# Clustered attention before two MLPs, one core: operands of the scores laid out as [hi; lo] and [hi; one-hot; maxima], and the first heads reordered

## Chip, core, metric

The kernel runs on one core of one Trainium2 chip. The metric is the device time of one execution in microseconds (us); lower is better.

## What is computed

Attention over 2 batches of 8 heads, 768 tokens, head size 64, where a query sees only keys of its own cluster, then two MLPs over the 1536 rows of 512 that the heads make together:

```python
q_assign = argmax(einsum('bhsd,hcd->bhsc', q_n, c_n), -1)   # nearest of 16 centroids of the head
k_assign = argmax(einsum('bhsd,hcd->bhsc', k_n, c_n), -1)
mask = q_assign[..., :, None] == k_assign[..., None, :]
scores = where(mask, scale * q @ k.T, -1e9)
attn = exp(scores - max(scores)); attn = attn / (sum(attn) + 1e-9)
x = (attn @ v) as rows of 512
h = x @ w_in;  x = (h * sigmoid(1.702 * h)) @ w_out                        # 2048 wide
out = (silu(x @ w_gate) * (x @ w_val)) @ w_out2                            # 1536 wide
```

All data are float32 in the reference; the kernel's inputs are laid out by the host without arithmetic.

## The kernel before

Every product on PE (TensorE) that must be accurate takes its operands as hi + lo, where hi carries the bits that one pass of the array keeps. Attention goes head by head, 16 heads; the two MLPs follow. Five pairs of operand tiles `q2`, `k2` go round among the heads, and a written-out order sets what each engine does (the scheduler keeps the program's order on all five engines).

What one head h needs, in the names used below:

- **Load and convert.** `load_qk` (L302) brings q and k, transposed, into a staging tile, twice over (one copy for the hi rows, one for the lo rows): 768 KB and 384 KB on the SP queue, two staging tiles. `hi_q`, `hi_k` (L319, L322) round them on ACT (ScalarE); `lo_q`, `lo_k` (L325, L329) take the difference, on DVE (VectorE) or, for the first heads, on POOL (GpSimd). This is done four heads ahead.
- **Clusters.** `similar` (L415): eight products per head of queries and keys with the centroids (`sims`). `largest` and `assign` (L440, L455): a chain of some nine operations on DVE that turns the similarities into one-hot rows, which are copied under the operands. From the fifth head on two heads go through it together.
- **Maxima.** `smax` (L490): 12 products and 12 reductions on DVE (`nm`), the largest score of each query; `mneg` (L508) and `mrow` (L525) or, for the first two heads, `mrow_at_once` (L512) put minus the maxima as a row under the queries, by a small transfer or by 6 tiny products and two copies on ACT.
- **Scores.** `scores` (L537): 12 pairs of products (`st`), each followed by Exp on ACT into `p`. Maxima of head h + 1 are mixed among them.
- **Values.** `pv` (L554): 36 products of `p` with the values (72 instructions), six at a time.

A score's first product takes 112 rows (hi and lo of half the sizes, one-hot rows at 96), its second 97 (the row of maxima at 96). `keep_warm` (L340, L344) issues products that nothing uses; they fill PE while it waits. The order of the first heads is in L606 to L634 and in the branches `if h == 0`, `if h == 1` of the loop over heads (L637 on): the one-hot chains of heads 0, 1, 2 and 3 go one head at a time.

Of the kernel before, what the change touches and what calls it, by code (L numbers as in the profile page):

```python
# [25 lines left out]
def tile_cluster_attention_two_mlps(ctx: ExitStack, tc: tile.TileContext, qk, v, cen, w1, w2, wg, wv, w3, out):  # L26
# [62 lines left out]
    # weights in the order of their first use  # L89
# [28 lines left out]
    def take_in():  # L118
        """Takes the weights in, one after the other, in steps of one operation of VectorE."""
# [18 lines left out]
    # the two MLPs, by parts of a batch's tokens  # L138
# [4 lines left out]
    def split_w(it):  # L143
        """A weight's split, as two thunks."""
# [26 lines left out]
    def first_products(b, f, p, names, tanh_scale):  # L171
        """Thunks: the first products of a part, through the activation."""
# [79 lines left out]
    def run(s1_thunks, splits, steps):  # L252
        """One part's or unit's thunks, the splits of later weights and `steps` of taking weights in, mixed."""
# [18 lines left out]
    with ExitStack() as att:  # attention  # L272
# [29 lines left out]
        def load_qk(h):  # L302
            b, hh = divmod(h, H)
            src = qk[b, hh].rearrange("d t s -> d (t s)")
            to = stage[h % 2].rearrange("p a t s -> p a (t s)")
            nc.sync.dma_start(out=to[0:64], in_=src.unsqueeze(1).to_broadcast([D, 2, 2 * S]))
            nc.sync.dma_start(out=to[64:96], in_=src.rearrange("(a p) s -> p a s", a=2))

        def load_first():
            src = qk[0, 0].rearrange("d t s -> d (t s)")  # L310
            to = stage[0].rearrange("p a t s -> p a (t s)")
            nc.sync.dma_start(out=to[0:64, 0], in_=src)
            nc.sync.dma_start(out=to[64:96], in_=src.rearrange("(a p) s -> p a s", a=2))
# [471 lines left out]
```

## Time and profile before

| what | value |
|---|---|
| timed runs | 870.86, 872.61, 872.85 us; median 872.61 us |
| profiled execution | span 869.7 us from its first to its last instruction; its time with what lies around the span is not listed apart |
| PE | busy 853.4 us (98%) |
| DVE, ACT, POOL | busy 605.8 us (70%), 431.9 us (50%), 30.9 us (4%) |
| granted clock of PE, mean | 0.991 |
| chain that ended last | PE 94%, DVE 4%, DMA 1% |
| loads of q and k | 15 issues of 768 KB and 17 of 384 KB; all traffic 61.92 MB |

The span runs from the first to the last instruction of the core. Attention takes about the first 300 us of it, the MLPs the rest. Busy time counts an engine's own instructions; PE's matmuls overlap, so that the start of one matmul after another tells its pace, not its duration. The granted clock of 1.00 is PE's upper level (2.4 GHz), 0.5 its lower (1.2 GHz); a stretch between them had some of both. Idle time of an engine is told with what ended it.

### The profile page before, as it was taken

The page shows a single profiled execution, that of the slowest core. Times are in us where ns is not written, and L with a number is a line of the kernel's source. Part 1 is how long each engine was busy: PE and PEld are TensorE (multiplying, and loading weights), DVE is VectorE, ACT ScalarE, POOL GpSimd, SP SyncE. Part 2 cuts the span into 40 slices and gives each one's busy share as a digit, 9 for nine tenths or more (in the row PEclk, how much of TensorE's full clock was granted, in tenths as well). Part 3 has the DMA queues.
Part 4 walks back from the last instruction along what each step waited for, and adds up shares of the span by engine and source line. Part 5 has one row for each costly group of instructions (what it writes and reads, how often), then busy time and mean ns, then how long its engine had stood idle before and what let it go on. Part 6 is the DMA issues. An engine that isn't in the chain of part 4 may idle for free.

```text
span 869.7 us, 12993 instructions
## 1 busy us (share of the span) xinstructions
PE 853.4 (98%) x5108; PEld 766.9 (88%) x5108; DVE 605.8 (70%) x1116; ACT 431.9 (50%) x809; POOL 30.9 (4%) x46
## 2 busy tenths in 40 slices
PE   6989999999999999999999999999999999999998
PEld 5789999999999888888888888888888888888886
DVE  7978889889897468888887677687773344334433
ACT  5645675575574555665665546454442233222322
POOL 5530000000000000000000000000000000000000
PEclk8989999999999999999999999999999999999999
DMA  7454633633122023323222222222200010000001
GB/s 160 105 119 114 150 99 91 154 70 91 46 63 88 5 73 109 110 100 120 98 98 73 74 83 73 87 74 72 97 1 1 1 49 25 1 1 1 0 1 73
DMA packets 28340, 61.92 MB, mean 71 GB/s; under 512 B 14756, under 2 KB 14840, under 8 KB 28280
## 3 DMA queue, kind: packets, MB, share of 16 engines
q1 hardware_dynamic: 27416, 59.53, 23.8%
q10 hardware_dynamic: 864, 1.57, 0.5%
q8 instruction: 40, 0.66, 0.3%
q14 instruction: 20, 0.16, 0.1%
HBM read 57.31 MB, written 3.15 MB: 70 GB/s over the span
## 4 chain that ended last, share of the span: by engine, by line
PE 94%; DVE 4%; DMA 1%; issue 0%; ACT 0%; SPq 0%; DVEq 0%
PE h L156 39%; PE a L156 27%; PE pv L559 14%; PE st L543 8%; PE smax L495 4%; PE sims L423 3%; PE xt L588 1%; DVE T L450 1%; DVE nm L500 1%; DMA st<-in_qk 1%; DVE T L452 0%; DVE q L389 0%; DVE oT L469 0%; DVE T L443 0%; DVE T L465 0%
## 5 line engine op out<-in xcount | busy, mean ns | idle before, releaser
L156 PE MATMUL h<-xh,sp 128*128 128x512 f32 (+1 forms) x1280 | 327.1, 337 | 0.1
L156 PEld LDWEIGHTS h<-xh,sp 128*128 128x128 f32 x1280 | 223.2, 189 | 28.5 <-issue 0.3
L156 PE MATMUL h<-xl,sp 128*128 128x256 f32 (+1 forms) x640 | 215.9, 337 | 0.0
L188 DVE SCALAR_TENSOR_TENSOR t<-t,h 128x512 f32<-128x512 f32 x112 | 61.8, 552 | 161.0 <-ACT t L185 161.0
L185 ACT ACTIVATE t<-h 128x512 f32<-128x512 f32 x112 | 54.7, 488 | 204.4 <-PE h L156 204.4
L156 PE MATMUL a<-g,sp 128*128 128x512 f32 (+1 forms) x768 | 139.4, 337 | 0.0
L156 PEld LDWEIGHTS a<-g,sp 128*128 128x128 f32 x768 | 119.9, 189 | 16.7
L559 PEld LDWEIGHTS pv<-v,p 128*128 128x128 f32 x1152 | 134.2, 192 | 0.2 <-issue 0.2
L559 PE MATMUL pv<-v,p 128*128 128x65 f32 x1152 | 133.9, 273 | 0.0
L156 PEld LDWEIGHTS h<-xl,sp 128*128 128x128 f32 x640 | 120.9, 189 | 14.3
L550 ACT ACTIVATE p<-st 128x384 f32<-128x384 f32 x192 | 90.8, 491 | 33.3 <-PE st L543 26.1
L156 PE MATMUL a<-sp,g 128*128 128x512 f32 x432 | 106.1, 390 | 0.0
L500 DVE TENSOR_REDUCE nm<-smax 128x1 f32<-128x384 f32 x192 | 100.1, 555 | 7.5 <-PE smax L495 7.4
L543 PE MATMUL st<-q,k 112*128 112x384 f32 (+1 forms) x384 | 100.3, 350 | 0.0
L150 DVE TENSOR_TENSOR sp<-w,sp 128x512 fp32r<-128x512 f32 x136 | 92.8, 684 | 5.2 <-ACT sp L149 5.1
L156 PEld LDWEIGHTS a<-sp,g 128*128 128x128 f32 x432 | 79.6, 188 | 15.6
L149 ACT CAST sp<-w 128x512 fp32r<-128x512 f32 x136 | 83.1, 614 | 0.0
L197 DVE TENSOR_TENSOR g<-t,g 128x512 fp32r<-128x512 f32 x112 | 62.0, 553 | 16.1 <-ACT g L194 11.5
L543 PEld LDWEIGHTS st<-q,k 112*128 112x128 f32 (+1 forms) x384 | 69.8, 193 | 1.9 <-ACT p L550 0.4
L495 PE MATMUL smax<-k,q 112*128 112x384 f32 x192 | 65.5, 351 | 5.3 <-ACT q L472 4.2
L194 ACT CAST g<-t 128x512 fp32r<-128x512 f32 (+1 forms) x48 | 24.7, 514 | 81.2 <-DVE t L193 81.2
L190 ACT CAST g<-t 128x512 fp32r<-128x512 f32 x64 | 32.9, 514 | 31.3 <-DVE t L188 31.3
(94 smaller groups left out, 687.4 us busy)
## 6 DMA issues: line engine op xcount, KB each, us to landing
raw<-in_w SPq DMA_DIRECT2D x44, 512.0 KB, 3.4
st<-in_qk SPq DMA_DIRECT2D x15, 768.0 KB, 6.1
st<-in_qk SPq DMA_DIRECT2D x17, 384.0 KB, 6.2
raw<-in_wg SPq DMA_DIRECT2D x12, 512.0 KB, 3.4
raw<-in_wv SPq DMA_DIRECT2D x12, 512.0 KB, 3.5
v<-in_v SPq DMA_DIRECT2D x16, 192.0 KB, 3.0
out<-osb ACTq DMA_DIRECT2D x6, 256.0 KB
out<-osb SPq DMA_DIRECT2D x6, 256.0 KB, 2.1
```

What stands on the lines that cost most here:

```text
L149: lambda: nc.scalar.copy(t[:, 0, :], w),
L150: lambda: nc.vector.tensor_tensor(out=t[:, 1, :], in0=w, in1=t[:, 0, :].bitcast(F32), op=ALU.subtract),
L156: nc.tensor.matmul(out=out_ps, lhsT=lhs[a], rhs=rhs[b], start=(start and j == 0), stop=(stop and j == 2), **kw)
L185: nc.scalar.activation(t, hs[0], ACTF.Tanh, scale=tanh_scale)
L188: nc.vector.scalar_tensor_tensor(out=t, in0=t, scalar=1.0, in1=hs[0], op0=ALU.add, op1=ALU.mult)
L190: nc.scalar.copy(g[:, 0, at], t)
L197: nc.vector.tensor_tensor(out=g[:, 1, at], in0=t, in1=g[:, 0, at].bitcast(F32), op=ALU.subtract)
L495: nc.tensor.matmul(out=ps, lhsT=q2(h)[:, 1, c * 128:(c + 1) * 128], rhs=k2(h)[:, 1, n * HALF:(n + 1) * HALF],)
L500: nc.vector.tensor_reduce(out=nm_t[h][:, c, n:n + 1], in_=ps, axis=AX.X, op=ALU.max)
L543: nc.tensor.matmul(out=ps, lhsT=k2(h)[0:rows, a, c * 128:(c + 1) * 128], rhs=q2(h)[0:rows, a, at], start=(a == 1), stop=(a == 0),)
L550: nc.scalar.activation(p_t[h, c][:, at], ps, ACTF.Exp, scale=scale)
L559: nc.tensor.matmul(out=pv_t[h][:, i, :], lhsT=p[:, i * 128:(i + 1) * 128], rhs=v_t[h % 3][:, c, :], start=(c == 0 and i == 0), stop=(c == ...
```

## The change

The operands are held in tiles of 128 rows. Slot 0 is [q_hi; q_lo] against [k_lo; k_hi], 64 rows each; slot 1 is [q_hi; one-hot at 64; zeros; row of maxima at 96] against [k_hi; one-hot; zeros; ones]. So a score is one product on 128 rows and one on 97; `smax` takes 80 rows of slot 1, and `sims` 128 rows in place of 96; the number of products is the same. Each head is loaded once (384 KB, one issue) into one of four staging tiles; head 0's q comes on the ACT queue. `hi_k` becomes two casts on ACT; `lo_q` is 64x768 where it was 32x1536. POOL clears rows 64 to 96 of slot 1 in all ten operand tiles (`extra_rows`). DVE sets `wd`, which POOL did.

The order of the first heads is written anew: head 0's maxima are taken in two halves, each followed at once by its row (`mrow_at_once(0, n)`) and half of head 0's scores; head 1's clusters come between the two halves; heads 2 and 3 go through the one-hot chain together, during head 0's products with the values; head 1's maxima row goes by the transfer. Two stretches of products that nothing uses are shorter or gone (20 to 16, 10 to none). `lo_q(4)` and `lo_k(4)` go to DVE, from POOL.

```diff
-        q2_t = [(qk1_p if i == FIRST else qk_p).tile([112, 2, S], F32R, name=f"q2_{i}") for i in range(NQK)]
-        stage = [st_p.tile([96, 2, 2, S], F32, name=f"st{i}") for i in range(2)]
+        q2_t = [(qk1_p if i == FIRST else qk_p).tile([128, 2, S], F32R, name=f"q2_{i}") for i in range(NQK)]
+        NST = 4
+        stage = [st_p.tile([D, 2, S], F32, name=f"st{i}") for i in range(NST)]
+        ONE, MROW = D, 96
...
         def load_qk(h):
-            nc.sync.dma_start(out=to[0:64], in_=src.unsqueeze(1).to_broadcast([D, 2, 2 * S]))
-            nc.sync.dma_start(out=to[64:96], in_=src.rearrange("(a p) s -> p a s", a=2))
+            nc.sync.dma_start(out=stage[h % NST], in_=qk[b, hh])
...
         def load_first():
+            for i, eng in ((1, nc.sync), (0, nc.scalar)):
+                eng.dma_start(out=stage[0][:, i, :], in_=qk[0, 0, :, i, :])
...
         def hi_q(h):
-            nc.scalar.copy(q2(h)[0:96], stage[h % 2][:, :, 0, :])
+            nc.scalar.copy(q2(h)[0:D], src.to_broadcast([D, 2, S]))
         def hi_k(h):
-            nc.scalar.copy(k2(h)[0:96], stage[h % 2][:, :, 1, :])
+            nc.scalar.copy(k2(h)[0:D, 1, :], src)
+            nc.scalar.copy(k2(h)[D:2 * D, 0, :], src)
...
+        def extra_rows(i):
+            for t in (q2_t[i], k2_t[i]):
+                nc.gpsimd.memset(t[D:MROW, 1, :].bitcast(F32), 0.0)
+            nc.gpsimd.memset(k2_t[i][MROW:MROW + 1, 1, :].bitcast(F32), 1.0)
...
         def scores(h, c, n):
-            for a, rows in ((1, 112), (0, 97)):
+            for a, rows in ((0, 2 * D), (1, MROW + 1)):
...
         sims = similar([0])
-        keep_warm(20)
+        keep_warm(16)
-        hi_q(1)
         hi_k(1)
-        lo_q(1, nc.gpsimd)
-        lo_k(1, nc.gpsimd)
-        load_qk(3)
+        hi_q(1)
         dummy = sm_p.tile([128, 1], F32, tag="dummy", name="dummy")
         nc.scalar.activation(dummy, y0, ACTF.Exp)
         do(largest([0], sims))
-        do(assign([0], (nc.scalar.copy, nc.vector.tensor_copy)))
-        hi_q(2)
+        do(assign([0], (nc.scalar.copy, nc.gpsimd.tensor_copy)))
+        lo_k(1, nc.gpsimd)
+        lo_q(1, nc.gpsimd)
         hi_k(2)
-        lo_q(2, nc.gpsimd)
+        extra_rows(2)
         lo_k(2, nc.gpsimd)
         load_qk(4)
         for i, (c, n) in enumerate((c, n) for m in range(2) for n in range(2) for c in range(3 * m, 3 * m + 3)):
             smax(0, c, n, *((ps_m, "m"), (ps_m, "m"), (ps_s, "s"), (ps_s, "s"), (ps_s, "s"))[i % 5])
-            if i == 4:
-                sims = similar([1])
-        mneg(0)
-        keep_warm(10)
-        mrow_at_once(0)
+            if i == 5:
+                mneg(0, slice(0, SC // 2))
+        mrow_at_once(0, 0, ps_o, "o")
+        mneg(0, slice(SC // 2, SC))
+        for c in range(SC):
+            scores(0, c, 0)
+        sims = similar([1])
+        mrow_at_once(0, 1, ps_o, "o")
         do(largest([1], sims))
-        do(assign([1], (nc.vector.tensor_copy, nc.vector.tensor_copy)))
+        do(assign([1], (nc.vector.tensor_copy, nc.gpsimd.tensor_copy)))
+        hi_q(2)
+        for c in range(SC):
+            scores(0, c, 1)
+        lo_q(2, nc.gpsimd)
+        hi_k(3)
+        lo_k(3, nc.gpsimd)
+        hi_q(3)
+        lo_q(3, nc.gpsimd)
+        for t in v_t[1:]:
+            nc.gpsimd.memset(t[:, :, D:D + 1], 1.0)
+        for i in range(3, NQK):
+            extra_rows(i)
         for h in range(NH):
...
-                        eng = nc.vector if h else nc.gpsimd
-                        lo_q(h + 4, eng)
-                        lo_k(h + 4, eng)
+                        lo_q(h + 4)
+                        lo_k(h + 4)
...
-                    if c == 2:
+                    if c == 3:
                         mneg(1)
-                        sims = similar([2])
-                        mrow_at_once(1)
-                        do(largest([2], sims))
-                        do(assign([2], (nc.scalar.copy, nc.vector.tensor_copy)))
-                if h == 1 and c == 1:
-                    do(largest([3], similar([3])))
-                    do(assign([3]))
+                        sims = similar([2, 3])
+                        mrow(1, ps_o, "o")
+                        do(largest([2, 3], sims))
+                        do(assign([2, 3]))
```

The order that comes of it, at three places. In the rows q_0 to q_4 and k_0 to k_4 are the operand tiles of heads 0 to 4 (and then of 5 to 9 again), st_120 to st_123 the staging tiles, and a row's x counts equal instructions that follow each other.

PE, from head 0's maxima to its products with the values, before:

```order
L495 MATMUL smax<-k_0_112,q_0_107 128x384 x7
L344 MATMUL warm<-xh_70 128x512 x10
L519 MATMUL mrow_348<-ident,nr 1x128 x3
L519 MATMUL mrow_353<-ident,nr 1x128 x3
L543 MATMUL st<-q_0_107,k_0_112 128x384 x14
L495 MATMUL smax<-k_1_113,q_1_108 128x384
```

and in the change:

```order
L353 MATMUL warm<-xh_70 128x512 x16
L502 MATMUL smax<-k_0_112,q_0_107 128x384 x12
L525 MATMUL mrow_319<-ident,nr 1x128 x3
L549 MATMUL st<-q_0_107,k_0_112 128x384 x12
L430 MATMUL sims<-k_1_113,cs 128x384 x2
L430 MATMUL sims<-q_1_108,cs 128x384 x2
```

Head 0's first scores stand right behind half of the row of maxima, and head 1's similarities, which stood between the maxima, behind those scores.

ACT, around head 0's Exps (L550, L556), before:

```order
L523 CAST q_0_107<-mrow_353 1x384
L550 ACTIVATE p<-st 128x384 x12
L320 CAST q_3_110<-st_121 96x1536
L323 CAST k_3_115<-st_121 96x1536
L320 CAST q_4_111<-st_120 96x1536
L323 CAST k_4_116<-st_120 96x1536
```

and in the change:

```order
L529 CAST q_0_107<-mrow_364 1x384
L321 CAST q_2_109<-st_122 64x1536
L556 ACTIVATE p<-st 128x384 x6
L325 CAST k_3_115<-st_123 64x768
L326 CAST k_3_115<-st_123 64x768
L321 CAST q_3_110<-st_123 64x1536
L321 CAST q_4_111<-st_120 64x1536
L325 CAST k_4_116<-st_120 64x768
L326 CAST k_4_116<-st_120 64x768
```

Head 2's `hi_q` now stands ahead of the second six Exps; the casts of heads 3 and 4 still follow the last Exp.

DVE, from head 1's one-hot rows to its maxima, before:

```order
L469 STREAM_TRANSPOSE oT<-T 64x384
L472 CAST q_1_108<-oT 16x384
L472 CAST k_1_113<-oT 16x384
L500 TENSOR_REDUCE nm<-smax 128x1 x12
L510 TENSOR_REDUCE nr<-nm 128x6
```

and in the change:

```order
L476 STREAM_TRANSPOSE oT<-T 64x384
L479 CAST q_1_108<-oT 16x384
L330 TENSOR_TENSOR q_4_111<-st_120,q_4_111 64x768
L336 TENSOR_TENSOR k_4_116<-st_120,k_4_116 64x768
L507 TENSOR_REDUCE nm<-smax 128x1 x12
L518 TENSOR_REDUCE nr<-nm 128x6
```

Head 4's `lo_q` and `lo_k` (L330, L336), which stood on POOL, now stand on DVE ahead of the 12 reductions of head 1's maxima.

## Rows read from the trace of the kernel before

**Rows 1.** Windows of the whole core: stretch, busy us (x instructions) by engine, clock, DMA share, GB/s.

```profile
50.00:55.00 5.00, 2.31 (x10) 1.97 (x10) 4.53 (x9) 1.62 (x4) 0.82 (x1) 0.77 1.11 215
55.00:60.00 5.00, 5.00 (x19) 5.00 (x18) 2.99 (x6) 2.59 (x6) 0.00 (x0) 0.55 0.69 143
...
100.00:150.00 50.00, 49.99 (x369) 49.55 (x367) 43.92 (x83) 30.97 (x55) 0.00 (x0) 1.00 0.47 117
...
200.00:250.00 50.00, 49.98 (x376) 49.64 (x374) 43.95 (x84) 31.02 (x55) 0.00 (x0) 1.00 0.22 56
```

**Rows 2.** Timeline of PE to 60 us: start, duration, line, work, idle before.

```profile
1.46 3.90 PE L344 MATMUL warm<-xh 128*128 128x512 f32 x9 [1.46 <-DVE y L348]
...
13.10 0.84 PE L423 MATMUL sims<-k,cs 96*128 96x384 f32 x2
13.74 0.84 PE L423 MATMUL sims<-q,cs 96*128 96x384 f32 x2
...
22.58 1.46 PE L495 MATMUL smax<-k,q 112*128 112x384 f32 x5 [1.52 <-ACT q L472]
...
29.46 1.47 PE L519 MATMUL mrow<-ident,nr 128*1 128x128 f32 x12
30.86 3.05 PE L543 MATMUL st<-q,k 112*128 112x384 f32 x14
...
38.12 1.45 PE L559 MATMUL pv<-v,p 128*128 128x65 f32 x12
...
53.43 0.69 PE L495 MATMUL smax<-k,q 112*128 112x384 f32 x1 [2.69 <-ACT q L472]
```

**Rows 3.** Timeline of PE from 60 us on.

```profile
64.88 0.59 PE L423 MATMUL sims<-k,cs 96*128 96x384 f32 x2
...
66.35 1.45 PE L559 MATMUL pv<-v,p 128*128 128x65 f32 x12
68.39 0.58 PE L423 MATMUL sims<-k,cs 96*128 96x384 f32 x2 [0.59 <-DVE T L443]
...
75.20 0.60 PE L543 MATMUL st<-q,k 112*128 112x384 f32 x2
...
83.01 6.86 PE L559 MATMUL pv<-v,p 128*128 128x65 f32 x60
```

**Rows 4.** Timeline of DVE to 62 us.

```profile
15.62 2.65 DVE L450 TENSOR_TENSOR T<-T,mx 128x192 f32<-128x192 f32 x1
18.38 1.81 DVE L452 TENSOR_TENSOR T<-T,wd 128x192 f32<-128x192 f32 x1
...
22.02 0.35 DVE L472 CAST k<-oT 16x384 fp32r<-16x384 f32 x1
...
23.40 5.66 DVE L500 TENSOR_REDUCE nm<-smax 128x1 f32<-128x384 f32 x12
...
30.79 0.36 DVE L452 TENSOR_TENSOR T<-T,wd 128x192 f32<-128x192 f32 x1
...
31.96 0.92 DVE L465 TENSOR_SCALAR T<-T,s,s 128x192 f32<-128x192 f32 x1
```

**Rows 5.** Timeline of POOL to 62 us.

```profile
14.60 3.46 POOL L327 TENSOR_TENSOR q<-st,q 32x1536 fp32r<-32x1536 f32 x1 [6.00 <-ACT q L320]
...
30.68 2.09 POOL L648 MEMSET k<- 1x768 f32 x3
```

**Rows 6.** Groups by line and shape: engine, work, count, busy us, mean ns, idle before.

```profile
L331 DVE TENSOR_TENSOR k<-st,k 64x768 fp32r<-64x768 f32 x11 | 10.5, 951 | 8.8 <-ACT k L323 8.7
L331 POOL TENSOR_TENSOR k<-st,k 64x768 fp32r<-64x768 f32 x5 | 9.1, 1819 | 0.6 <-ACT k L387 0.3
...
L480 ACT CAST k<-oT 16x768 fp32r<-16x768 f32 x6 | 5.0, 829 | 0.1
...
L450 DVE TENSOR_TENSOR T<-T,mx 128x384 f32<-128x384 f32 x6 | 3.3, 558 | 0.2
...
L387 ACT CAST k<-st 64x1536 fp32r<-64x1536 f32 x1 | 1.5, 1476 | 1.1 <-DMA st<-in_qk 1.1
```

More of the change, by code (lines that the diff above doesn't have):

```diff
@@ L337, in tile_cluster_attention_two_mlps @@
         load_v(0)
+        load_qk(2)
+        load_qk(3)
         zeros = xh[0][:, 0, 0:512]
@@ L379, in tile_cluster_attention_two_mlps @@
         nc.vector.reciprocal(y1, y1)
-        cn = acst.tile([128, 2, 96], F32, name="cn")
-        for a in range(2):
-            nc.vector.tensor_scalar(out=cn[:, a, 0:64], in0=craw, scalar1=y1, scalar2=None, op0=ALU.mult)
-            nc.vector.tensor_scalar(
-                out=cn[:, a, 64:96], in0=craw[:, 32 * a:32 * a + 32], scalar1=y1, scalar2=None, op0=ALU.mult
-            )
-        first = stage[0][0:64, 0:1]
-        nc.scalar.copy(k2(0)[0:64], first[:, :, 1, :].to_broadcast([64, 2, S]))
@@ L388, in tile_cluster_attention_two_mlps @@
-        nc.scalar.copy(q2(0)[0:64], first[:, :, 0, :].to_broadcast([64, 2, S]))
-        nc.vector.tensor_copy(q2(0)[64:96], stage[0][64:96, :, 0, :])
-        lo_k(0, nc.gpsimd)
-        ctp = ps_x.tile([96, 2, 128], F32, tag="x", name="ctp")
-        keep_warm(9)
-        for a in range(2):
-            nc.tensor.transpose(out=ctp[:, a, :], in_=cn[:, a, :], identity=ident)
-        ch = acst.tile([96, 2, 128], F32R, name="ch")
-        cl = acst.tile([96, 2, 128], F32R, name="cl")
+        cn = acst.tile([128, 2, D], F32, name="cn")
@@ new lines, in tile_cluster_attention_two_mlps @@
+        nc.vector.tensor_scalar(
+            out=cn, in0=craw.unsqueeze(1).to_broadcast([128, 2, D]), scalar1=y1, scalar2=None, op0=ALU.mult
+        )
+        ctp = ps_x.tile([128, 128], F32, tag="x", name="ctp")
+        keep_warm(9)
+        nc.tensor.transpose(out=ctp, in_=cn.rearrange("p a d -> p (a d)"), identity=ident)
+        keep_warm(5)
+        ks, qs = stage[0][:, 1, :], stage[0][:, 0, :]
+        nc.vector.tensor_copy(k2(0)[0:D, 1, :], ks)
+        nc.scalar.copy(q2(0)[0:D, 0, :], qs)
@@ L408, in tile_cluster_attention_two_mlps @@
-        for n in range(2):
-            at = slice(n * HALF, (n + 1) * HALF)
-            t = q2(0)[64:96, :, at]
-            nc.vector.tensor_tensor(out=t, in0=stage[0][64:96, :, 0, at], in1=t.bitcast(F32), op=ALU.subtract)
+        for i, src, r in ((0, ch, slice(0, 2 * D)), (1, cl, slice(0, D)), (2, cl, slice(D, 2 * D))):
+            to = cs[r, i, LEAD:].rearrange("p (h x) -> p h x", x=128)[:, :, 0:NC]
+            nc.scalar.copy(to, src[r].rearrange("p (h c) -> p h c", c=NC))
+        lo_k(0)
@@ L412, in tile_cluster_attention_two_mlps @@
+        lo_q(0)
+        nc.scalar.copy(q2(0)[0:D, 1, :], qs)
         ident_r = acst.tile([128, 128], F32R, name="ident_r")
@@ L531, in mrow @@
             nc.sync.dma_start(
-                out=q2(h)[96:97, 0, :].rearrange("p (c s) -> p c s", s=128).bitcast(F32), in_=row.bitcast(F32)
+                out=q2(h)[MROW:MROW + 1, 1, :].rearrange("p (c s) -> p c s", s=128).bitcast(F32), in_=row.bitcast(F32)
             )
@@ L546, in scores @@
                     rhs=q2(h)[0:rows, a, at],
-                    start=(a == 1),
-                    stop=(a == 0),
+                    start=(a == 0),
+                    stop=(a == 1),
                 )
@@ L639, in tile_cluster_attention_two_mlps @@
             maxima = list(steps) if more else []
-            for i, step in enumerate(steps):
+            for step in steps if h else ():
                 scores(h, *step)
-                if maxima and (h > 0 or i >= 6):
+                if maxima:
                     next_smax(h + 1, maxima)
             if h == 0:
-                for t in v_t[1:]:
-                    nc.gpsimd.memset(t[:, :, D:D + 1], 1.0)
-                for t in k2_t[2:]:
-                    nc.gpsimd.memset(t[96:97, 0, :].bitcast(F32), 1.0)
-                hi_q(3)
-                hi_k(3)
-                lo_q(3, nc.gpsimd)
-                lo_k(3, nc.gpsimd)
                 load_qk(5)
```

96 lines of the change are left out of this document (44 added, 52 removed).

## Prediction

> **What bounds the kernel now.** I read the windows of the core first, then PE's timeline, then DVE's and POOL's timelines where PE waits, then the groups for durations. From 100 us on PE is busy 49.99 of 50 us [rows 1]: there it sets the pace and waits for nobody, and the change leaves its number of products alone. So what the change is worth lies before, up to head 2's first score, at 75.20 us [rows 3]; behind it I move the rest of the kernel as one block. Up to there PE's timeline shows what holds it: head 0's maxima start at 22.58, its scores at 30.86, its products with the values at 38.12, head 2's maxima at 53.43 after 2.69 us idle [rows 2]. The profiled span is 869.7 us; that execution's own time isn't listed, and the median of the runs, 872.61, stands 2.9 above the span. I keep that distance and forecast by the shift of the 75.20. A difference of 0.3%, about what can be told from none, is 2.6 us.
>
> **The steady part: nothing.** Per head `hi_k` is two casts of 0.83 us on ACT for one of 1.48, `lo_q` on DVE goes to 0.95 (rows of the same shape as `lo_k` now) [rows 6]: both engines have room beside PE (31 and 44 of 50 us [rows 1]). Where that cover were gone, ACT's 0.2 us a head would be 3 us in all. The loads fall to a third, but PE doesn't wait for them.
>
> **Head 0 to its first score.** PE's nine fillers end at 5.36 [rows 2], a transposition and three short DVE operations follow; I estimate four times 0.35, the cast of [rows 4]: 6.8. Then `lo_k`, `lo_q`, 0.95 each [rows 6]: 8.7. Six of the eight similarities wait for them; at 0.18 each (1.47 for eight, 64.88 to 66.35 [rows 3]) the chain on DVE starts at 10.1. Before, it was 14.6 (13.74 + 0.84 [rows 2]). The chain took 7.4 us to the first cast at 22.02, because two of its operations took 2.65 and 1.81 where such a one takes 0.36 [rows 4]. POOL's subtraction ran from 14.60 to 18.06, and the first of them ended at 18.27 [rows 5, 4]: DVE was held till POOL's instruction was done. The change puts POOL's subtractions behind the chain: 7.4 - 3.7 = 3.7, to 13.8. The first half's cast for k is now POOL's; no row shows one, so between DVE's 0.35 and half of POOL's subtraction of twice the size, 0.91 [rows 4, 6]; I take 0.6 (it reads one operand, not two). The second half is 0.6 later, but the first maxima need the first alone: start at 14.6, 8.0 us early. Reductions go at 0.47 (5.66 for 12 [rows 4]); the first ends near 15.4, and the small reduction after six, the seventh, and the last product that needs its buffer bring 18.8. Half a row of maxima is 0.73 (1.47 for both [rows 2]), its copy on ACT 0.5 by an estimate from 0.83 for twice the columns [rows 6]: **scores from 20.0, where it was 30.86, a lead of 10.9 us.**
>
> **The beginning's new work on POOL.** The memset of rows 64 to 96 is three times 0.70 for each pair of tiles [rows 5], two pairs of them ahead of the chain, beside DVE's first operations. Beside such memsets a DVE operation with two inputs took 0.36, as always, and one with a single input and scalars 0.92, ending 0.1 after the memset [rows 4, 5]. So I charge `lo_k`, `lo_q` nothing and the copy of k0 at most 0.7, which the fillers on PE cover in part. Were all held, 2.1 us would be added to the 14.6. The Trainium skill, SBUF — State Buffer, section "Who interferes with whom", says the same with a reason: a VectorE instruction with two SBUF inputs is kept off by a GpSimd one that reads SBUF, not by one that only writes, and one in a two-port mode by either. By that rule the sum stays as it is without the 2.1, and the rule speaks against the change further on: subtractions of both engines exclude each other.
>
> **Head 0's scores and values.** Six pairs at 0.436 (3.05 for seven [rows 2]): 22.6. Head 1's similarities 1.47: 24.1. The second half of the row, 0.73, and its copy: 25.3. On ACT `hi_q(2)` stands in front of the second Exps, 1.48 [rows 6]: 26.8, and six Exps at the pairs' pace end at 29.4. PE's last pair is out at 28.5; values from 28.5, where it was 38.12: lead 9.6.
>
> **The new wait.** DVE's 12 reductions for head 1 stand behind `lo_q(4)`, `lo_k(4)`, and these behind ACT's casts: after the last Exp k(3), two of 0.83, q(3) and q(4), 1.48 each, to 34.0 [rows 6]. POOL, free at 30.2 after its last cast, does three subtractions of 1.82 [rows 6], to 35.7; its third and DVE's `lo_q(4)` want the same moment, and one waits for the other as in [rows 4, 5]. Either way three operations follow each other from 33.8: 1.82 + 2 x 0.95 = 3.7, **37.5**. Had they not excluded each other, 35.9. PE meanwhile does six products of `pv` with 12 instructions at 0.11 (6.86 for 60 [rows 3]), three maxima, six more, and stops at 31.7 for want of a PSUM buffer till the first reduction ends, 38.0: **6.3 us idle, where before nothing stopped here.**
>
> **Heads 1 to 3.** Reductions to 43.3 or so (12 x 0.47), mneg, 16 similarities 2.9: 46.4. The chain for two heads at once is nine operations at 0.56 [rows 6]: 51.6; two casts of 0.83: head 2's maxima at 53.5. Before: 53.43. **The lead is spent.** PE has two blocks of values, the row and a pair of scores to do after the similarities, some 3.1 us, so it idles 4 us. The SP queue isn't late: head 1's row goes out behind `load_qk(6)`, which waits for POOL's `lo_q(2)` near 32 and is past by 46. From 53.43 to 75.20 before passed 21.8 us, in them head 3's similarities of their own (1.47) and a wait for DVE's buffer, 0.59 [rows 3], which are gone: 19.7.
>
> **The clock.** After the 2.69 us idle at 53.4 the granted clock was 0.77 and 0.55 in two stretches of 5 us [rows 1]: 2.3 + 4.5 = 6.8 us at the lower level of 1.2 GHz. There pairs stand 0.64 apart (13.10 to 13.74 [rows 2]), 0.36 at the upper. The change's second gap, 4 us, should bring the same: already in the 19.7. Its first, 6.3 us, has none to match. Behind it reductions bind at first, then 16 similarities and values that would double. At most half of 6.8 is lost, 3.4; at least 0, if only work beside DVE meets it. I take 2.5, nearer to the upper end, since the similarities alone would lose 2.9.
>
> **Sum.** 53.5 + 2.5 + 19.7 = 75.7 against 75.20: +0.5, less the rounding of 0.1, 872.6 + 0.4 = **873.0 us**. The lead of 10.9 goes as 1.3 (`hi_q(2)` and the similarities between the halves), 6.3 (the new wait), the rest to the joint chain and the clock, against 2.1 won back.
>
> **Rivals.**
> - *Faster: the clock stays up behind both gaps.* For it: the rows show the effect of one gap alone. Against: that one was 2.69, shorter than either of these. Worth 2.5, and 3.0 in head 1's scores and maxima (6.8 us hold seven threes of products at 0.96, which take 0.53 at the upper level): 867.5; with one of them 870.
> - *Slower: a third fall, between 15 and 28 us.* PE does 12 maxima at the reductions' pace, then waits for a copy, scores at the Exps' pace, another copy: some 9.4 us of work in 14. Before, 30 fillers stood here, now 16. If the lower level is granted when the scores start, six pairs lose 0.2 each, similarities 1.1, the tiny products 0.7: 3.0, 876.0; with the first gap's full 3.4, 877. It decides once the scores' pairs stand over 0.5 apart. Against: before, behind 12 maxima at like paces, pairs still stood 0.436 apart at 30.86 [rows 2].
> - *The change doesn't act where it says:* fewer bytes or full rows quicken all of attention. In the window with a DMA share of 0.22 there are 376 products, in that with 0.47 369 [rows 1]. If loads and not the mix of products made that 2%, halving the traffic of some 200 us would give 2 us: 870.6. Against: PE waits for no load in either.
>
> **How the numbers follow.** Forecast 0.53; third fall 0.22; clock up 0.18; quicker products 0.07. The low end takes from 75.7 the first gap's 2.5, 1.6 for subtractions that don't exclude each other: 71.6, and rounds the cast: 868.5, with the case of both gaps at the upper level beyond it. The high end adds 3.0, 0.9 and 0.3 for each of two POOL casts: 877.5. Outside lie some 2 in 10. Faster by over 0.3%: most of the clock case and a little of the last, 0.20. Slower: the third fall and the upper edge of the forecast, 0.25. Within: 0.55.
>
> **What would show it.** Right: the first score near 20 us; on PE a gap of 4 to 7 us before head 1's fourth maximum, ended by DVE's reduction, with `lo_q(4)` and `lo_k(4)` just ahead of it; head 2's first maximum near 54 to 56 after a second gap of some 4 us; clock under 1.00 behind both; from head 2 on PE busy as before. Wrong: no such gap (then some 6 us faster), the chain on DVE still held by POOL, PE idle after 80 us, or matmuls of another pace at 100 to 300 us.

## The result, and the profile after

| | before | after |
|---|---|---|
| timed runs, median | 872.59 us (4 runs, 870.86 to 872.85) | 877.52 us (4 runs, 874.94 to 877.55) |
| ratio of the runs | 1 | 1.0061, 95% interval 1.0042 to 1.0080 |
| profiled execution, span | 869.7 us | 875.6 us (its own time: 877.51) |
| mean granted clock | 0.991 | 0.980 |
| PE, DVE busy | 853.4, 605.8 us | 857.8, 583.8 us |

The change makes the kernel slower by 0.6%, where 873.0 and "within 0.3%" were forecast; 877.52 lies just beyond the upper end of the range, 877.5. Runs of one kernel differ with the clock that they were granted (the changed kernel took 877.5 us three times at a mean of 0.980 and 874.94 once at 0.984), so that a difference of two medians below is good to some 1 to 2 us. The 5.9 us of span come from the beginning: head 2's first score is 6.95 us later, and behind it the kernel is quicker by about 1. PE's timeline of the changed kernel (start, duration, line, work, idle before) tells where:

```profile
14.15 4.74 PE L502 MATMUL smax<-k,q 80*128 80x384 f32 x12 [0.77 <-ACT q L479]
18.82 1.44 PE L525 MATMUL mrow<-ident,nr 128*1 128x128 f32 x6
20.18 4.82 PE L549 MATMUL st<-q,k 128*128 128x384 f32 x12
24.80 0.84 PE L430 MATMUL sims<-k,cs 128*128 128x384 f32 x2
...
32.14 1.45 PE L565 MATMUL pv<-v,p 128*128 128x65 f32 x12
...
40.98 1.62 PE L502 MATMUL smax<-k,q 80*128 80x384 f32 x3 [5.53 <-DVE nm L507]
42.39 2.66 PE L565 MATMUL pv<-v,p 128*128 128x65 f32 x12
...
62.51 0.69 PE L502 MATMUL smax<-k,q 80*128 80x384 f32 x1 [4.04 <-ACT k L487]
...
82.15 0.60 PE L549 MATMUL st<-q,k 128*128 128x384 f32 x2
```

Against [rows 2]: head 0's maxima start at 14.15 (22.58), its scores at 20.18 (30.86), its values at 32.14 (38.12), head 2's maxima at 62.51 (53.43); against [rows 3], head 2's scores at 82.15 (75.20). A lead of 10.7 us at the scores is 6.0 at the values and minus 9.1 at head 2's maxima. Two waits stand on the way, 5.53 and 4.04 us, and something that is no wait: 12 score products take 4.82 us (14 took 3.05 before), a block of values 2.66 where it took 1.45. The windows (busy us and instructions by engine, granted clock, DMA share, GB/s) say what that is:

```profile
15.00:20.00 5.00, 4.85 (x15) 2.09 (x13) 4.97 (x13) 1.25 (x2) 4.87 (x5) 0.73 0.09 21
20.00:25.00 5.00, 5.00 (x15) 4.03 (x14) 0.62 (x3) 2.93 (x6) 2.31 (x2) 0.50 0.49 98
25.00:30.00 5.00, 4.81 (x21) 3.50 (x19) 2.22 (x6) 2.09 (x3) 0.00 (x0) 0.74 0.00 0
...
35.00:40.00 5.00, 0.45 (x4) 0.31 (x3) 2.67 (x2) 3.83 (x4) 4.81 (x6) 0.78 0.28 79
40.00:45.00 5.00, 4.03 (x16) 3.67 (x17) 3.24 (x7) 0.00 (x0) 3.20 (x5) 0.50 0.00 0
45.00:50.00 5.00, 4.63 (x19) 4.12 (x18) 2.46 (x6) 0.00 (x0) 0.00 (x0) 0.50 0.00 0
50.00:55.00 5.00, 4.89 (x16) 4.89 (x17) 0.68 (x3) 0.00 (x0) 0.00 (x0) 0.51 0.00 0
...
100.00:150.00 50.00, 49.97 (x371) 49.70 (x370) 40.96 (x80) 33.37 (x60) 0.00 (x0) 1.00 0.26 70
```

A window at clock 0.73 has 2 x (1 - 0.73) x 5 = 2.7 us at the lower level of 1.2 GHz. So PE was there for 2.7 + 5 + 2.6 = 10.3 us around 20 us, with no long idle ahead of it, and for 2.2 + 5 + 5 + 4.9 = 17.1 us from within the first wait on (3.2 of them still in the wait, 13.9 behind it). Before, the stretch at the 2.69 us idle had 6.8 [rows 1]. The last row answers to the 100 to 150 of [rows 1]: 371 products for 369, DMA share 0.26 for 0.47.

The first wait's cause, in DVE's timeline and (last row) POOL's:

```profile
37.30 2.17 DVE L330 TENSOR_TENSOR q<-st,q 64x768 fp32r<-64x768 f32 x1 [4.66 <-ACT q L321]
39.50 0.95 DVE L336 TENSOR_TENSOR k<-st,k 64x768 fp32r<-64x768 f32 x1
40.38 2.87 DVE L507 TENSOR_REDUCE nm<-smax 128x1 f32<-128x384 f32 x6
```

```profile
36.85 1.80 POOL L330 TENSOR_TENSOR q<-st,q 64x768 fp32r<-64x768 f32 x1
```

`lo_q(4)` waits 4.66 us for ACT's cast, then lasts 2.17 where `lo_k(4)` takes 0.95: POOL's subtraction, from 36.85, ends at 38.65, and DVE's ends 0.82 later. Head 1's reductions (`nm`) stand behind both in DVE's queue and start at 40.38; PE's next maximum waits for the first of them.

### The profile page after: what moved, and what is told of

It is laid out like the page before. It is cut to its first block, busy times and chain, and to the rows that moved or that the text cites. A ratio compares the mean times of both kernels' runs of the same rounds, so it can differ in the third digit from the quotient of the medians.

```text
span 875.6 us, 12903 instructions
## 1 busy us (share of the span) xinstructions
PE 857.8 (98%) x5082; PEld 770.4 (88%) x5082; DVE 583.8 (67%) x1114; ACT 431.5 (49%) x815; POOL 28.6 (3%) x43
## 4 chain that ended last, share of the span: by engine, by line
PE 94%; DVE 3%; ACT 1%; issue 0%; DMA 0%; DVEq 0%; ACTq 0%; SPq 0%
PE h L156 38%; PE a L156 27%; PE pv L565 13%; PE st L549 7%; PE smax L502 4%; PE sims L430 3%; DVE nm L507 1%; PE xt L594 1%; ACT q L321 0%; PE warm L353 0%; DVE q L330 0%; DVE oT L476 0%; ACT p L556 0%; PE mrow L525 0%; DMA q<-oT 0%
## 5 line engine op out<-in xcount | busy, mean ns | idle before, releaser
L565 PEld LDWEIGHTS pv<-v,p 128*128 128x128 f32 x1152 | 136.8, 195 | 0.1
L565 PE MATMUL pv<-v,p 128*128 128x65 f32 x1152 | 136.3, 276 | 0.0
L556 ACT ACTIVATE p<-st 128x384 f32<-128x384 f32 x192 | 91.0, 491 | 37.9 <-PE st L549 30.7
L549 PE MATMUL st<-q,k 128*128 128x384 f32 (+1 forms) x384 | 102.3, 356 | 1.1 <-ACT p L556 0.9
L502 PE MATMUL smax<-k,q 80*128 80x384 f32 x192 | 67.7, 365 | 10.5 <-DVE nm L507 5.5
L549 PEld LDWEIGHTS st<-q,k 128*128 128x128 f32 (+1 forms) x384 | 71.5, 199 | 4.3 <-ACT p L556 1.8
L502 PEld LDWEIGHTS smax<-k,q 80*128 80x128 f32 x192 | 38.2, 202 | 14.0 <-DVE nm L507 8.1
```

The source lines that it names most:

```text
L502: nc.tensor.matmul(out=ps, lhsT=q2(h)[0:ONE + NC, 1, c * 128:(c + 1) * 128], rhs=k2(h)[0:ONE + NC, 1, n * HALF:(n + 1) * HALF],)
L549: nc.tensor.matmul(out=ps, lhsT=k2(h)[0:rows, a, c * 128:(c + 1) * 128], rhs=q2(h)[0:rows, a, at], start=(a == 0), stop=(a == 1),)
L556: nc.scalar.activation(p_t[h, c][:, at], ps, ACTF.Exp, scale=scale)
L565: nc.tensor.matmul(out=pv_t[h][:, i, :], lhsT=p[:, i * 128:(i + 1) * 128], rhs=v_t[h % 3][:, c, :], start=(c == 0 and i == 0), stop=(c == ...
```

## The experiments

Theory A: the time went to the wait at 35 to 41 us and, more than to it, to the lower clock behind it and around 20 us. Theory B: to the wait alone. Theory C: to the joint chain of heads 2 and 3. Theory D: to the layout on full rows. Ten kernels were run, each in four runs (e2 in ten), beside the kernel before, whose median was then 871.69 us (beside e1, e2, e3 and e5), 871.63 (e6 to e9) and 871.46 (e10, e11); the ratios are to these.

| kernel | median, us | ratio to before, 95% interval | head 2's first score, us | span behind it, us |
|---|---|---|---|---|
| before | 872.59 | | 75.20 | 794.5 |
| after | 877.52 | 1.0061, 1.0042 to 1.0080 | 82.15 | 793.4 |
| e1 | 867.62 | 0.9953, 0.9938 to 0.9968 | 71.74 | 793.7 |
| e2 | 871.47 | 1.0015, 0.9997 to 1.0032 | 75.92 | 793.7 |
| e3 | 858.16 | 0.9852, 0.9835 to 0.9868 | 62.04 | 793.6 |
| e5 | 874.48 | 1.0040, 1.0026 to 1.0055 | 79.28 | 793.3 |
| e6 | 865.80 | 0.9933, 0.9916 to 0.9949 | 69.55 | 793.5 |
| e7 | 863.78 | 0.9908, 0.9893 to 0.9923 | 67.56 | 793.5 |
| e8 | 864.88 | 0.9916, 0.9902 to 0.9931 | 69.63 | 793.7 |
| e9 | 855.65 | 0.9815, 0.9800 to 0.9830 | 60.11 | 793.9 |
| e10 | 862.94 | 0.9902, 0.9886 to 0.9919 | 66.99 | 793.7 |
| e11 | 857.65 | 0.9841, 0.9824 to 0.9857 | 62.62 | 793.9 |

The last column is the profiled span less the column before it. It hardly moves, so every kernel below is decided before head 2's first score.

### e1: the wait taken away

```diff
-                        lo_q(h + 4)
-                        lo_k(h + 4)
+                        eng = nc.vector if h else nc.gpsimd
+                        lo_q(h + 4, eng)
+                        lo_k(h + 4, eng)
```

> Edit: the changed kernel, but head 4's two subtractions (lo_q(4), lo_k(4)) go back from VectorE to GpSimd, so head 1's reductions no longer stand behind them. Theory A (the wait of 5.5 us and the lower clock behind it, 37 to 54 us, are what the time went to): no idle of over 1 us before head 1's fourth maximum, granted clock 1.00 from 30 to 45 us, head 2's first maximum near 50 us (62.5 in the changed kernel), 865 us (863 to 868). Theory B (the wait alone, with no part of the clock): 5.5 less, 872 us (871 to 873). Theory C (the joint chain of heads 2 and 3 sets the end whatever comes ahead): 876 to 878. Theory D (the layout on full rows costs time by itself, all along): 876 to 878, with the gap gone all the same.

Measured 867.62 us. PE's timeline of e1:

```profile
34.93 0.77 PE L502 MATMUL smax<-k,q 80*128 80x384 f32 x3
...
40.20 0.88 PE L430 MATMUL sims<-k,cs 128*128 128x384 f32 x2 [0.77 <-DVE nm L507]
...
52.65 0.69 PE L502 MATMUL smax<-k,q 80*128 80x384 f32 x1 [4.68 <-ACT k L487]
```

The wait is gone (the fourth maximum, at 34.93, follows the values without idle time) and the time falls by 9.9 us, more than the 5.5 of the wait. B (872), C and D (876 to 878) fall, each as the one cause; A's range holds it. Head 2's maxima came at 52.65, not near 50: the clock was 0.66 at 40 to 45 us, so part of the similarities still went at the lower level.

### e2: the wait kept, PE kept busy in it

```diff
             for c in range(SC):
                 pv(h, c)
+                if h == 0 and c == 1:
+                    keep_warm(22, ps_s, "s")
```

(`keep_warm` is given the pool of its buffer as an argument.)

> Edit: the changed kernel with 22 products that nothing uses (128x512) on TensorE right behind the second block of head 0's products with the values, where TensorE waits 5.5 us for VectorE. VectorE's wait stays as it is; TensorE is busy in it. Theory A: granted clock 1.00 from 37 to 54 us, so the products behind the wait go at their upper pace, head 2's first maximum near 56 us and 871 us (869.5 to 872.5). Theory B (the wait alone, no part of the clock) and theory D (layout): no change, 877.5 us (876.5 to 879). If the products that nothing uses last longer than the wait, up to 1 us more in every theory.

Measured 871.47 us. PE's timeline of e2:

```profile
35.13 5.28 PE L353 MATMUL warm<-xh 128*128 128x512 f32 x22
40.95 1.37 PE L502 MATMUL smax<-k,q 80*128 80x384 f32 x3 [0.54 <-DVE nm L507]
42.16 1.45 PE L565 MATMUL pv<-v,p 128*128 128x65 f32 x12
...
57.05 0.69 PE L502 MATMUL smax<-k,q 80*128 80x384 f32 x1 [4.04 <-ACT k L487]
```

This parts the wait from the clock. The fourth maximum starts at 40.95, in the changed kernel at 40.98: DVE's wait is untouched. But the next block of values takes 1.45 for 2.66, head 2's maxima come 5.5 us sooner, and 6.05 us are gone from the median. That is what the lower clock behind the first idle cost: 6.05, not the 2.5 of the forecast. The figure holds for the executions whose rows stand here (877.51 and 871.52 us, 5.99 apart). Four of the ten runs of e2 took 875.2 to 876.1 us, and no trace shows where they lost it; by the means of all runs the gain is 4.0 us, which is still above the 3.4 that the forecast called the most. e1 takes another 3.85 us off: the wait of 5.5, less what e1 loses again to the lower clock at 40 to 45 us and to its longer second idle (4.68 for 4.04).

### e3: the new layout in the old order

The order of L606 to L634 and of the branches `h == 0`, `h == 1` is put back, on the new tiles, loads and setup. The rows that matter:

```diff
+        lo_q(1, nc.gpsimd)
+        lo_k(1, nc.gpsimd)
         do(largest([0], sims))
...
+            if i == 4:
+                sims = similar([1])
-        mrow_at_once(0, 0, ps_o, "o")
+        mneg(0)
+        keep_warm(10)
+        mrow_at_once(0, 0, ps_s, "s")
+        mrow_at_once(0, 1, ps_s, "s")
...
+                if maxima and (h > 0 or i >= 6):
+                    next_smax(h + 1, maxima)
...
-                    if c == 3:
+                    if c == 2:
                         mneg(1)
-                        sims = similar([2, 3])
+                        sims = similar([2])
```

> Edit: the changed kernel's layout, loads and setup, with the order of the first heads as it was before (both halves of the maxima's row at once, 10 unused products ahead of them, heads 2 and 3 one at a time, head 4's subtractions on GpSimd, heads 1 to 3 split as before). Theory A (the new order with its wait and the clock cost the time, the layout and the quicker setup none): the setup's lead of some 5 us stays, 868 us (866 to 872.5). Theory D (the layout on full rows costs time by itself): 876 us or more. Theory C (the joint chain of heads 2 and 3): below 872.5 as well, so this run parts only D from the others.

Measured 858.16 us: 13.5 below before, 19.4 below the change, and below the range given. PE's timeline of e3:

```profile
16.64 1.35 PE L502 MATMUL smax<-k,q 80*128 80x384 f32 x5 [2.19 <-ACT q L479]
...
24.82 3.04 PE L549 MATMUL st<-q,k 128*128 128x384 f32 x14
...
43.80 0.34 PE L502 MATMUL smax<-k,q 80*128 80x384 f32 x1
```

D falls for good: in the old order full rows, single loads and the quicker setup are a gain of 13.5 us (no run parts the three), and the rebuilt order throws it away and 5.8 more. Head 0's first score comes 4.6 us later than in the changed kernel, head 2's first maximum 18.7 us sooner, with no idle ahead of it. The granted clock was 1.00 in every window from 5 to 85 us. Of the 13.2 us against before at head 2's first score, 6.0 are there at head 0's (24.82 for 30.86), 3.6 come between that and head 2's first maximum, where the 2.69 us idle is gone, and 3.5 behind it, with the lower clock gone: from head 2's first maximum to its first score 18.2 us for 21.8.

Why the idle is gone stands in the one-hot chain of head 2. DVE's and (last row) POOL's timeline of before:

```profile
45.81 3.34 DVE L450 TENSOR_TENSOR T<-T,mx 128x192 f32<-128x192 f32 x1
49.18 1.85 DVE L452 TENSOR_TENSOR T<-T,wd 128x192 f32<-128x192 f32 x1
```

```profile
45.51 3.43 POOL L327 TENSOR_TENSOR q<-st,q 32x1536 fp32r<-32x1536 f32 x1
```

and of e3 (DVE):

```profile
39.05 0.36 DVE L457 TENSOR_TENSOR T<-T,mx 128x192 f32<-128x192 f32 x1
39.44 0.36 DVE L459 TENSOR_TENSOR T<-T,wd 128x192 f32<-128x192 f32 x1
```

Beside POOL's subtractions for head 4 two operations of the chain took 5.2 us for 0.7, 4.5 more, which is more than the whole idle; in e3 POOL does the memsets of `extra_rows` at that time (37.15 to 41.67). So part of e3's gain is a matter of what POOL does while this chain runs.

### e5: the lower clock around 20 us taken away

```diff
             smax(0, c, n, *((ps_m, "m"), (ps_m, "m"), (ps_s, "s"), (ps_s, "s"), (ps_s, "s"))[i % 5])
+            keep_warm(1)
...
         mrow_at_once(0, 0, ps_o, "o")
+        keep_warm(6)
```

> Edit: the changed kernel with one product that nothing uses behind each of head 0's 12 maxima and six behind the first half of the maxima's row; nothing else. Theory A (thin work between 14 and 19 us lets the clock fall to the lower level, 16.7 to 26.9 us, and that costs 3.5 to 4): granted clock 1.00 from 15 to 30 us, head 0's first six pairs of scores in 2.7 us instead of 4.8, 873.5 us (872.5 to 875), the later gap of 5.5 us and its clock as they were. If the later wait took this lead up (its end set by something else than head 0's scores): 877.5 us. Should the unused products be in the way: up to 879.

Measured 874.48 us, 3.04 less. PE's timeline of e5:

```profile
21.63 2.48 PE L549 MATMUL st<-q,k 128*128 128x384 f32 x12
23.95 0.52 PE L430 MATMUL sims<-k,cs 128*128 128x384 f32 x2
...
38.91 1.62 PE L502 MATMUL smax<-k,q 80*128 80x384 f32 x3 [5.54 <-DVE nm L507]
```

The 18 unused products put the first score off by 1.45 us, and head 1's similarities still start 0.85 sooner, because 12 score products take 2.48 for 4.82. The wait behind is as long as it was, 5.54, and ends 2.1 sooner. This is the rival with a third fall of the clock, which was priced at 3.0; the 3.04 are what is left after the 1.45 that the unused products take.

### e6, e10, e7: the parts together, and the second wait

e6 is e1 and e5 together. e10 is e6 with PE kept busy in the second wait:

```diff
                 scores(h, *step)
+                if h == 1 and step == (0, 0):
+                    keep_warm(22, ps_s, "s")
```

e7 is e6 with heads 2 and 3 through the chain one at a time:

```diff
-                        sims = similar([2, 3])
+                        sims = similar([2])
                         mrow(1, ps_o, "o")
-                        do(largest([2, 3], sims))
-                        do(assign([2, 3]))
+                        do(largest([2], sims))
+                        do(assign([2], (nc.scalar.copy, nc.vector.tensor_copy)))
+                if h == 1 and c == 1:
+                    do(largest([3], similar([3])))
+                    do(assign([3]))
```

> Edit: the edits of e1 and e5 together (head 4's subtractions on GpSimd, and the unused products behind head 0's maxima and the row). Theory A: head 0's first values near 30.1 us as in e5 (31.8 in e1), no lower clock between 15 and 45 us, the second idle of over 4 us as in e1 with its lower clock; 865.5 us (863.5 to 867). If the lead of e5 is taken up by a later wait once the first one is gone: 867.5, as e1.

> Edit: e6 with 22 products that nothing uses behind head 1's first pair of scores, where e6's TensorE waits 5.8 us for head 2's one-hot row; the wait itself stays. Theory A (each such idle costs its length and, behind it, a stretch at the lower clock): granted clock 1.00 throughout from 15 us on, the threes of scores and maxima behind the wait 0.53 apart instead of 0.96, some 3 us less than e6: 862.8 us (861.8 to 864). If the clock behind the second idle costs nothing at the end: 865.8, as e6.

> Edit: e6, and heads 2 and 3 get their one-hot rows one at a time as before (head 2 behind head 0's fourth block of values, head 3 behind head 1's second). Theory A, with the joint chain as the third part: the chain for one head is some 3 us shorter (eight fewer similarities ahead of it, one operation less per half, copies by halves), so the idle ahead of head 2's maxima falls from over 4 to 1 to 2 us; if the clock then stays up, 860 us (858 to 862), if it falls all the same, 862.5. If the joint chain is no cost (its idle would only come elsewhere): as e6, 865.5.

Measured 865.80, 862.94 and 863.78 us. e6 is 1.8 us quicker than e1, for e5's 3.0. At 40 to 45 us e1's clock had been 0.66, e6's is 1.00, though both do the same work ahead of it; no run shows why. But the idle ahead of head 2's maxima grew from 4.68 to 5.83. DVE's timeline of e6 shows by what:

```profile
43.15 2.05 DVE L459 TENSOR_TENSOR T<-T,wd 128x384 f32<-128x384 f32 x1
```

Two operations of the joint chain took 0.86 and 2.05 us beside POOL's subtractions for head 4, where such a one takes 0.56: 1.8 us more, in e1 0.65. The difference is the 1.15 us by which the idle grew. PE's timeline of e10:

```profile
44.02 5.17 PE L353 MATMUL warm<-xh 128*128 128x512 f32 x22
50.03 0.45 PE L502 MATMUL smax<-k,q 80*128 80x384 f32 x1 [0.85 <-ACT k L487]
50.31 0.52 PE L549 MATMUL st<-q,k 128*128 128x384 f32 x2
...
50.85 0.51 PE L549 MATMUL st<-q,k 128*128 128x384 f32 x2
```

Head 2's maxima start at 50.03 (e6: 49.98), so that wait is untouched too; the pairs behind it come 0.54 apart and 2.9 us are gone. e7 gained 2.0 over e6, short of the 3 to 5.5 expected: PE in e7 is still idle for 3.77 us ahead of head 2's maxima (46.87), and its clock was 0.50 at 45 to 50 us. DVE's and (last row) POOL's timeline of e7:

```profile
41.40 1.91 DVE L459 TENSOR_TENSOR T<-T,wd 128x192 f32<-128x192 f32 x1
43.74 1.45 DVE L470 TENSOR_TENSOR T<-T,mx 128x192 f32<-128x192 f32 x1
```

```profile
41.29 1.80 POOL L330 TENSOR_TENSOR q<-st,q 64x768 fp32r<-64x768 f32 x1
```

Two operations took 3.36 us for 0.72 beside POOL's subtractions for head 4: 2.6 of the 3.77 us. One head at a time is not enough while these stand beside the chain; e7 stays 5.6 us above e3.

### e8: the joint chain alone, in the old order

```diff
                     if c == 2:
                         mneg(1)
-                        sims = similar([2])
+                        sims = similar([2, 3])
...
-                        do(largest([2], sims))
-                        do(assign([2], (nc.scalar.copy, nc.vector.tensor_copy)))
-                if h == 1 and c == 1:
-                    do(largest([3], similar([3])))
-                    do(assign([3]))
+                        do(largest([2, 3], sims))
+                        do(assign([2, 3]))
```

> Edit: e3 (the old order, the new layout), with one thing of the new order put in: heads 2 and 3 get their one-hot rows in one chain behind head 0's third block of values. Theory A: TensorE has three blocks of values and two scores, some 4.5 us, for the similarities' chain of some 9 us: idle 3 to 4 us ahead of head 2's maxima, clock at the lower level behind it, 863 us (861 to 866). If the joint chain is no cost in an order without other waits: 858 (857 to 859).

Measured 864.88 us, 6.7 above e3. PE's timeline of e8:

```profile
16.84 1.43 PE L502 MATMUL smax<-k,q 80*128 80x384 f32 x5 [2.90 <-ACT q L479]
18.06 0.84 PE L430 MATMUL sims<-k,cs 128*128 128x384 f32 x2
...
26.37 3.04 PE L549 MATMUL st<-q,k 128*128 128x384 f32 x14
...
50.40 0.69 PE L502 MATMUL smax<-k,q 80*128 80x384 f32 x1 [3.41 <-ACT k L487]
```

Three things are in it. With the joint chain PE is idle for 3.41 us where e3 had no idle, and the clock is lower at it. But the chain was also held, as in e6 and e7. DVE's and (last row) POOL's timeline of e8:

```profile
44.03 1.46 DVE L470 TENSOR_TENSOR T<-T,mx 128x384 f32<-128x384 f32 x1
45.53 1.85 DVE L472 TENSOR_SCALAR T<-T,s,s 128x384 f32<-128x384 f32 x1
```

```profile
45.15 2.01 POOL L336 TENSOR_TENSOR k<-st,k 64x768 fp32r<-64x768 f32 x1
```

In the changed kernel, where POOL stands idle beside the joint chain, the two took 0.56 and 0.48. So 2.3 of the 3.41 us are POOL's subtractions. And the beginning, which has the same program as e3's, fell to the lower level too (similarities 0.64 apart at 18 us), behind an idle of 2.90 for e3's 2.19 (one operation of head 0's chain took 1.84 us beside POOL's subtraction, in e3 1.14); it puts the first score at 26.37 for 24.82, 1.55 us. At head 2's first score e8 is 7.6 behind e3; the 6.0 that are left are the joint chain together with what held it. What the joint chain costs alone no run shows.

### e9 and e11: a version that beats both

e9 is e3 with what gave the new order its lead, and with PE kept busy. Against e3:

```diff
-        keep_warm(20)
+        keep_warm(16)
...
+        do(assign([0], (nc.scalar.copy, nc.gpsimd.tensor_copy)))
+        lo_k(1, nc.gpsimd)
+        lo_q(1, nc.gpsimd)
...
+            if i < 6:
+                keep_warm(1)
+            if i == 5:
+                mneg(0, slice(0, SC // 2))
-            if i == 4:
+            if i == 8:
                 sims = similar([1])
-        mneg(0)
-        keep_warm(10)
-        mrow_at_once(0, 0, ps_s, "s")
-        mrow_at_once(0, 1, ps_s, "s")
+        mrow_at_once(0, 0, ps_o, "o")
+        keep_warm(5)
+        mneg(0, slice(SC // 2, SC))
+        for c in range(SC):
+            scores(0, c, 0)
+        mrow_at_once(0, 1, ps_o, "o")
```

Head 0's second half of scores is then mixed with head 1's first six maxima. e11 is e9 without `keep_warm(1)` and `keep_warm(5)`.

> Edit: e3 with the parts of the new order that gave head 0 its lead and none of those that took it: GpSimd's subtractions behind head 0's chain, one cast of each half on GpSimd, the row of maxima by halves with the first half's scores ahead, 11 unused products in place of 10 (six of them between maxima); head 1's similarities behind head 0's ninth maximum. Theory A (nothing but the start is early or late once TensorE is kept busy): head 0's first score at 20.2 us instead of 24.8, of which some 1 us is lost again to the copy of the second half; 854.5 us (853 to 857). If the lead is taken up by head 1's chain, which starts no earlier than its reductions let it: 857 to 858.5. If a thin stretch lets the clock fall: 860 or more.

> Edit: e9 without its 11 unused products between head 0's maxima and behind the first half of the maxima's row; the 16 ahead of the maxima stay. Theory A (thin work there lets the clock fall, as in the changed kernel at 16.7 us): a lower stretch beginning between 15 and 25 us, head 0's pairs of scores 0.64 apart for some 7 us, 859 us (857.5 to 861). If head 1's eight similarities, which now stand between the maxima, are work enough: clock 1.00, 855 (854 to 856).

Measured 855.65 us (e9) and 857.65 us (e11). PE's timeline of e9:

```profile
18.46 0.61 PE L430 MATMUL sims<-q,cs 128*128 128x384 f32 x2 [0.73 <-POOL q L330]
...
22.25 2.48 PE L549 MATMUL st<-q,k 128*128 128x384 f32 x12
```

The first score came at 22.25, not 20.2: head 1's similarities stand between the maxima, wait 0.73 us for POOL's `lo_q(1)` and take 1.5 themselves, and five of the unused products (1.3 us) stand right ahead of the score. Against e3 2.5 us are left of the 4.6 that were looked for. The window of e11 behind its maxima,

```profile
20.00:25.00 5.00, 5.00 (x17) 3.44 (x16) 3.70 (x10) 0.97 (x3) 4.17 (x5) 0.50 0.82 171
```

is at the lower level: the 11 unused products are worth 2.0 us, less than the 3.4 that the 859 expected would have meant. e9 is the quickest kernel here, 0.9815 (0.9800 to 0.9830) of before.

## Why the prediction was wrong

**Right: the setup and head 0's first score.** The chain on DVE was to start at 10.1 and not be held by POOL; it started at 9.78, with its operations at 0.35 to 0.38. First score 20.0 forecast, 20.18 measured. That it is so close is in part luck: the maxima started 0.45 us sooner than forecast (14.15 for 14.6), and half the row of maxima, already at the lower clock, took 0.7 longer (1.44 us for 0.73). Beside POOL's memsets head 0's `lo_k`, a subtraction with two inputs, took 0.94 us; `lo_q(4)` was held by POOL's subtraction until that ended (2.17 for 0.95 us); in e3, where POOL's subtractions stand beside head 0's chain again, two of its operations took 1.14 and 1.88 us for 0.36. These traces agree with the rule of the Trainium skill, SBUF — State Buffer, section "Who interferes with whom", that the prediction drew on.

**Right: the new wait and the joint chain.** A gap of 6.3 us before head 1's fourth maximum was forecast, with `lo_q(4)` and `lo_k(4)` ahead of it; it is 5.53. POOL's last subtraction and DVE's two were to follow each other within 3.7 us; they took 3.6 (36.85 to 40.45). A second gap of 4 us; it is 4.04. From head 2's first maximum to its first score 19.7; it is 82.15 - 62.51 = 19.6.

**Wrong: the step "The clock".** It charged the first gap's lower stretch 2.5 us, at most 3.4, half of the 6.8 us that the lower level had lasted at the 2.69 us idle of before. e2 measures this term: 6.05 us (4.0 by the means of all runs). The stretch lasted 17.1 us. Behind the gap PE did blocks of values, threes of maxima and then 16 similarities, all at the lower level, and the chain of reductions, similarities and clusters runs through them. The ends of that step's range were drawn from the length of one other stretch, which bounds nothing about this one. Nor was it the only stretch in the rows, as the first rival has it ("the effect of one gap alone"): before shows another at 10 to 20 us, from which the step itself took its 0.64. The windows of before:

```profile
10.00:15.00 5.00, 3.45 (x10) 2.90 (x11) 3.62 (x6) 4.33 (x10) 0.40 (x1) 0.67 1.11 208
15.00:20.00 5.00, 5.00 (x17) 3.92 (x16) 4.82 (x4) 2.32 (x3) 4.92 (x3) 0.65 0.60 125
```

That is 3.3 + 3.5 = 6.8 us at the lower level, with an idle of 4.18 us that ended at 11.45. It too was no measure of the 17.1.

**Wrong: the third fall put at nothing.** It was a rival at 0.22, priced 3.0, and not in the sum; it happened, from some 17 us on, and e5 measures 3.04. That the price fits is luck: the first 12 score products alone lost 2.3 us (4.62 us to the similarities behind them, in e5 2.32) for the 1.2 that were priced, and e5's figure is less the 1.45 us of its unused products. Against the rival stood that pairs of scores before were still 0.436 apart behind 12 maxima; but before, eight similarities stood among those maxima and ten unused products behind them, and the change moved the ones and struck out the others. e11 shows the same: without unused products there the clock fell even with the similarities in place. The row was not comparable, and the diff said why.

The two together are 3.55 + 3.04 = 6.6 us; head 2's first score was forecast at 75.7 and came at 82.15, 6.45 late. What reached the median is less, for two smaller reasons. The span behind head 2's first score is 793.3 to 793.9 us in eleven traces of the new layout and 794.5 in the one of before, so the steady part is quicker by about 1 us, in the direction of the rival priced at 2 (one trace of before does not settle its size). And the 2.9 us put between span and time was too much: the changed kernel's profiled execution has 877.51 - 875.6 = 1.9, as its other runs do; the 869.7 belonged to an execution below its median.

**What was not asked.** Forecast and rivals weighed layout and order as one. e3 shows them apart: layout and setup -13.5 us, the order +19.4. One path from the changed kernel towards e3 adds up: e1 9.9 us (6.05 the clock behind the first wait, 3.85 the rest of the wait), e6 another 1.8 (what is left there of the clock around 20 us, 3.04 while the wait stands), e10 another 2.9 (the clock at the second wait). The 4.8 us left to e3 are not parted by a run; e10 still has the second wait, filled with 5.2 us of unused products, and e3 has none. Why e7 stays 5.6 above e3 is read from the timelines, not tried by itself: POOL's subtractions held its chain for 2.6 us where e3's stood beside memsets, and in e7 all 12 of head 1's maxima come with the values, in e3 six among head 0's scores, so that e3's chain has one more block of values (1.25 us) to cover it. The forecast had reckoned with this exclusion in head 0's chain and for `lo_q(4)` alone; the longest operations of the chain in before, 3.34 and 1.85 us at 45.8 to 51 us, were in the timeline that it read.

## What to carry to other kernels

Price an idle of TensorE as its length plus what the work behind it loses at the lower clock, and don't take that loss from the length of some other lower stretch: here that was 6.8 us, and at the gap in question 17.1. Unused products in the gap, with the wait left as it is, part the two costs in one run. In the chain that PE waits for, look for operations that take several times their usual length, and at what another engine does beside them: subtractions on POOL made 4.5 us of before's chain, 2.6 of e7's and 2.3 of e8's. And where a change brings a layout and an order together, run the new layout in the old order first: a lead at the first head is worth nothing if a later engine's queue hands it to a wait.

## What was not expected of the hardware

- The lower level lasted 6.8 us at idles of 2.69 (before), 3.41 (e8: 1.3 + 5 + 0.5 from its windows) and 3.77 us (e7: 0.1 + 5 + 1.7), 10.2 at 5.83 (e6: 4.3 + 5 + 0.9), 17.1 at 5.53 (after) and 5.54 (e5: 0.4 + 15 + 1.7). It began within each of these idles; counted from their ends it is 6.1, 5.1, 4.8 and 5.9 us for the first four, 13.9 and 12.8 for the last two. The idle's length doesn't order them. Behind the first four PE did pairs of scores with a maximum each, behind the last two blocks of values, threes of maxima and similarities, and it was busy there, 4.63 and 4.89 us of 5 (after, 45 to 55 us). Why the clock took so long to rise no run tells.
- The clock fell with no long idle: from 14.15 us on the changed kernel's PE lists none behind the first 0.77, but 15 products in 15 to 20 us where e5 has 28, and the clock in that window was 0.73 for e5's 1.00. In e1 it fell at some 40 us at an idle of 0.77 (0.66 in 40 to 45 us), where e6 with the same work and the same idle kept 1.00.
- The same program at the beginning stayed at the upper level behind an idle of 2.19 us (e3) and fell behind one of 2.90 (e8).
- A subtraction on POOL held not only DVE's operations with two inputs but also one with a single input and scalars (e8: 1.85 us for 0.48); its memsets left the operations with two inputs at 0.36 (e3).
